# Attention and two MoE layers on one core: float32r scores for 50 of 80 items, an earlier load of block 2, logits a step later

## The chip, the cores and the metric

One core of a Trainium2 chip runs the whole program. The metric is the time of one execution in device microseconds. Before the change the median of three runs is 1098.74 us (1095.99 to 1099.82).

Engines are called by these names: TensorE (PE in the profile; PEld is its weight load, which overlaps), VectorE (DVE), ScalarE (ACT), GpSimd (POOL) and SyncE (SP), whose queue issues most of the DMA transfers. Each engine works through its own queue in order.

## What is computed

Three layers in a row, on 4 x 576 = 2304 tokens with 512 features, everything in float32:

```python
# attention, 4 batches x 8 heads x 576 tokens x 64
scores = q @ k.T / 8 + bias            # bias[h, i, j]: a small MLP of log1p|i-j| / log1p(max(i, 1))
attn = softmax(scores)                 # sums + 1e-9
x = attn @ v                           # laid out as 2304 x 512
# first MoE layer: dense, 512 -> 2048 -> 512
h = x @ w_in
y = (h * clip(h + 3, 0, 6) / 6) @ w_out
# second MoE layer: each token to the one of 8 experts with the largest logit
e = argmax(y @ w_gate)
out = gate * sigmoid(y @ w_output_gate)[e] * (relu(y @ w1[e]) @ w2[e])
```

## The kernel before, in words

**Attention.** The work is cut into 80 items. An item is a pair of heads (pr), of a unit u (a batch and four of its heads; 8 units), for a chunk c of query rows (64 rows, then four chunks of 128). Units 0 to 2 come first, interleaved over the chunks, with the computation of the bias between them (items 0 to 29). Units 3 to 7 follow, one after the other, 10 items each (items 30 to 79). A software pipeline of steps works on several items at once: `Attn.emit` writes for each step s the scores of item s (`qk`, Q0 and Q1, lines 313 to 330), the exponentials of item s-1 (`sm_exp`, line 336), its normalization (`sm_norm`, lines 342 to 345), the transposes of item s-3 (`pv_tr`, line 358, copied out of PSUM in lines 361 and 363) and the product with V of item s-4 (`pv`, lines 373 to 380, stored to `xT_d` in line 380). The order within a step is a string, `T0 S T1 X0 X1 Q0 Q1 P N T2`; at S all that was hung on this step with `side[s]` is issued: loads of q (`load_q`, line 306), K (`load_k`, line 299), V, and pieces of the MoE that start early.

The scores are fp32 matmuls, line 325: K and q of two heads lie in partitions 0 to 63 and 64 to 127, so one head uses the upper and one the lower 64 rows of the array (`tile_position=(64 * i, 0)`); each has two halves of 288 columns. Line 328 adds the bias on VectorE and takes the row's minimum of the negated scores.

**First MoE layer.** Tokens come in nine blocks of 256 (`NB`). Its matrices are held as pairs of float32r values: a high part (a copy that rounds to float32r, on ScalarE) and a low part (the subtraction, on VectorE), and each product is three float32r matmuls, high x high, high x low and low x high. The weights w_in and w_out arrive as 32 pieces of 64-bit numbers (`w_load`, line 576), each turned into such a pair by `w_steps` in four parts a to d (lines 603, 606, 609 and 610, 613 and 614). Pieces 0 to 3 are converted during attention (`w_early`, at steps 36 + 8p and the four after), the rest in `tick`, called from the loop over the matmul groups. `w_c` of piece p starts loads up to piece p+3. A block's rows are loaded by `x_load` (line 638) and split by `x_prep` (lines 656 and 657; for block 2 lines 649 and 650). `l1_` is a group of 12 matmuls of 256 columns (line 671) and its activation (lines 677 to 683), `l2_` six matmuls of 512 columns (line 701). Blocks 0 to 2 run interleaved, `seq` holding the order; groups 0 and 1 are issued already within the attention's last steps (`next(gen)`).

**Routing.** `tail` gives six parts per block: copy y out (line 714), two transposes (line 724, copied in line 725), the logits (line 730), their transposition and gate (line 738 on), the position in the expert's table (line 763 on). `tails(b, g, steps)` hangs them on matmul groups, one number of `steps` for each.

**Second MoE layer.** Slots of 128 tokens of one expert, again with float32r pairs (lines 1024 and 1052); the change doesn't touch it.

Buffers are named by tags, and a new tile under a tag waits until the tile before has been read. Tags that matter here: `K0` to `K2`, `V0` to `V2`, `xb0` to `xb3`, `cv`, `e0` to `e4` (softmax rows), `xo0` and `xo1` (attention output ahead of its store), `qh0`, `qh1`, `ql0`, `ql1`, `qraw`, `r0` and `r1`.

## Time and profile before

| | |
|---|---|
| median of three runs | 1098.74 us |
| the profiled execution | 1101.62 us |
| its span, first to last instruction | 1099.9 us |
| mean granted TensorE clock | 0.984 |
| TensorE busy | 1050.7 us (96%) |
| VectorE busy | 617.7 us (56%) |
| ScalarE busy | 539.5 us (49%) |
| GpSimd busy | 221.0 us (20%) |

The profile records one execution. "Busy" of TensorE counts from a matmul's start to its modelled end, so that matmuls which follow each other closely overlap; how fast they follow is seen from their starts in the timeline. A row of the timeline gives start, duration, engine, line and operation of one or several instructions of a kind (x8: eight of them from the first start to the last end), and in brackets the idle time of the engine before and what ended it. Attention lasts to about 386 us, the first MoE layer to about 815 us, the second to the end.

### The profile page before, as it was taken

Reading aid. Unit: us, or ns where it says so; the run is one execution under the profiler, and the core shown is the slowest. Engines: PE = TensorE matmul, PEld = TensorE weight load, DVE = VectorE, ACT = ScalarE, POOL = GpSimd, SP = SyncE. Lnnn points to the kernel's source line nnn. Section 1 sums busy time; section 2 is a strip of 40 time slices with the busy share of each in tenths; the row PEclk is TensorE's granted clock in tenths of the full one; section 3 lists DMA queues with packets and bytes.
Section 4 is the critical chain, followed back from the end, with each engine's and each line's share of the span. In section 5 each row is a group of like instructions: output and inputs, shape, how many; then the busy total and the mean of one; then the engine's idle time right before and its main releaser. Section 6 shows DMA issues by size and latency. Waiting matters only on the chain. (4 is left out here: it accounts for less than half of the span.)

```text
span 1099.9 us, 20984 instructions
## 1 busy us (share of the span) xinstructions
PE 1050.7 (96%) x7637; PEld 818.7 (74%) x7637; DVE 617.7 (56%) x1554; ACT 539.5 (49%) x1198; POOL 221.0 (20%) x273
## 2 busy tenths in 40 slices
PE   5999999999999979999999999999999989999996
PEld 2355556767777769988788888898887868777774
DVE  4887865667776757776454443436355624345320
ACT  4678777667776644554333333333343123354421
POOL 0132323434444300000010000001311243221111
PEclk9999999999999989999999999999999989999998
DMA  7555481323232143431102010110421265677841
GB/s 233 173 192 171 155 281 50 107 77 97 76 95 75 52 127 113 124 126 58 58 21 39 1 39 1 39 39 2 136 77 33 56 234 209 236 291 278 330 160 38
DMA packets 62192, 129.19 MB, mean 117 GB/s; under 512 B 13820, under 2 KB 35708, under 8 KB 59264
## 3 DMA queue, kind: packets, MB, share of 16 engines
q1 hardware_dynamic: 57424, 117.69, 32.3%
q0 software_dynamic: 4512, 9.49, 3.0%
q8 instruction: 62, 1.02, 0.4%
q10 hardware_dynamic: 144, 0.59, 0.3%
q14 instruction: 50, 0.41, 0.2%
HBM read 164.08 MB, written 14.65 MB: 163 GB/s over the span
## 5 line engine op out<-in xcount | busy, mean ns | idle before, releaser
L701 PE MATMUL acc<-wp,g 128*128 128x512 f32 x864 | 227.3, 398 | 2.1 <-issue 1.7
L671 PE MATMUL ph<-xh,wp 128*128 128x256 f32 x1024 | 207.3, 285 | 1.4 <-ACT y L714 1.2
L701 PEld LDWEIGHTS acc<-wp,g 128*128 128x128 f32 x864 | 154.4, 190 | 29.4 <-issue 2.1
L345 POOL TENSOR_SCALAR e<-e,st 128x576 f32<-128x576 f32 (+1 forms) x160 | 126.2, 801 | 246.0 <-DVE st L343 177.0
L671 PEld LDWEIGHTS ph<-xh,wp 128*128 128x128 f32 x1024 | 167.0, 189 | 11.0 <-issue 3.7
L328 DVE CUSTOM_DVE_ANT_0 e<-sc,bias 128x576 f32<-128x576 f32 (+1 forms) x160 | 116.4, 751 | 63.6 <-PE sc L325 60.9
L671 PE MATMUL ph<-xl,wp 128*128 128x256 f32 x512 | 144.6, 282 | 0.7 <-issue 0.4
L677 ACT ACTIVATE r<-ph,small 128x256 f32<-128x256 f32 x144 | 67.4, 468 | 128.8 <-PE ph L671 124.3
L336 ACT ACTIVATE e<-e,st 128x576 f32<-128x576 f32 (+1 forms) x160 | 123.0, 776 | 0.0
L678 DVE SCALAR_TENSOR_TENSOR t<-r,ph 128x256 f32<-128x256 f32 x144 | 60.3, 419 | 109.8 <-ACT r L677 109.7
L680 ACT ACTIVATE g<-t 128x256 fp32r<-128x256 f32 x144 | 60.2, 418 | 115.0 <-DVE t L678 114.0
L1024 PE MATMUL peh<-ws,xt 128*128 128x512 f32 x408 | 102.7, 405 | 5.1 <-PEq L1334 5.0
L325 PE MATMUL sc<-K,q 64*128 64x288 f32 (+1 forms) x640 | 103.0, 432 | 0.1
L358 PE MATMUL pt<-cst,e 128*128 128x128 f32 (+1 forms) x720 | 97.5, 268 | 2.9 <-ACT eT L361 1.8
L671 PEld LDWEIGHTS ph<-xl,wp 128*128 128x128 f32 x512 | 97.0, 189 | 4.1 <-DVE xl L657 0.5
L358 PEld LDWEIGHTS pt<-cst,e 128*128 128x128 f32 (+1 forms) x720 | 75.8, 141 | 31.7 <-issue 14.1
L775 POOL DMA_INDIRECT tab_d<-small x18 | 18.2, 1008 | 387.6 <-DVE small L773 353.0
L1024 PEld LDWEIGHTS peh<-ws,xt 128*128 128x128 f32 x408 | 76.9, 192 | 23.1 <-issue 5.7
L683 DVE SCALAR_TENSOR_TENSOR g<-t,g 128x256 fp32r<-128x256 f32 x144 | 61.1, 424 | 56.1 <-ACT g L680 56.1
L1052 PE MATMUL peo<-ws,ehh 128*128 128x512 f32 x272 | 86.1, 398 | 0.0
L373 PEld LDWEIGHTS po<-eT,V 128*64 128x64 f32 x1280 | 64.0, 138 | 24.8 <-issue 17.4
L373 PE MATMUL po<-eT,V 128*64 128x128 f32 (+1 forms) x1280 | 81.9, 271 | 0.0
(215 smaller groups left out, 1454.5 us busy)
## 6 DMA issues: line engine op xcount, KB each, us to landing
er<-in_we SPq DMA_DIRECT2D x46, 1024.0 KB
er<-in_we SPq DMA_DIRECT2D x86, 512.0 KB
xb<-in_xb SPq DMA_DIRECT2D x38, 512.0 KB
wraw<-in_wf SPq DMA_DIRECT2D x32, 512.0 KB
cv<-in_xb SPq DMA_DIRECT2D x11, 512.0 KB
K<-in_kT SPq DMA_DIRECT2D x8, 576.0 KB
xr<-xT_d SPq DMA_DIRECT2D x9, 512.0 KB
y_d<-y SPq DMA_DIRECT2D x18, 256.0 KB
```

The source lines that it names most:

```text
L325: nc.tensor.matmul(self.sc[i][:R, n, :288], q[d, pr, :], self.kv[u][d, pr, n * 288:(n + 1) * 288], start=True, stop=True, tile_position=(6 ...
L328: nc.vector.tensor_tensor_reduce(out=e[:R, j, :].rearrange("p (n s) -> p n s", n=2), in0=self.sc[j][:R, :, :288], in1=self.bias[c][:R, 4 * ...
L336: self.nc.scalar.activation(e[:R, j, :], e[:R, j, :], AF.Exp, scale=-1.0, bias=st[:R, j:j + 1], accum_out=st[:R, 4 + j:5 + j])
L345: nc.gpsimd.tensor_scalar(e[:R, j, :], e[:R, j, :], st[:R, 6 + j:7 + j], 1.0, op0=ALU.mult, op1=ALU.mult)
L358: nc.tensor.transpose(pt[:, i, :R], src[3 * gi + i], self.ident[:R, :R])
L373: nc.tensor.matmul(po[64 * j:64 * j + 64, :], vm[:, 2 * pr + j, kb, :], eT[:, 2 * kb + j, :], start=kb == 0, stop=False, tile_position=(0, ...
L671: nc.tensor.matmul(ph, w, x[c], start=n == 0, stop=n == 11)
L677: nc.scalar.activation(r, ph, AF.Relu, bias=self.three)
L683: nc.vector.scalar_tensor_tensor(g[:, 1], t, 1.0 / 6.0, g[:, 0].bitcast(F32), op0=ALU.mult, op1=ALU.subtract)
L701: nc.tensor.matmul(acc[t], x, w, start=f == 0 and i == 0, stop=f == 15 and i == 2)
L1024: nc.tensor.matmul(ph[:, n, :], a, w, start=c == 0 and i == 0, stop=c == 3 and i == 2)
L1052: nc.tensor.matmul(d["po"], a, w, start=f == 0 and i == 0, stop=f == 7 and i == 2)
```

## The change

The scores of units 3 to 7 (50 of the 80 items) are made of three float32r products. K and q of these units are loaded into raw buffers; `prep_k` and `prep_q` split them into high and low parts, with a copy on ScalarE and a subtraction on VectorE. K of unit 3 is loaded two steps earlier than before and split in steps 28 and 29, that of the others five and four steps ahead of their first item; q is split one step ahead of its use, from a single raw buffer, and the next load of q is issued right behind.

The rows of block 2 are loaded at step 73 together with those of blocks 0 and 1, into `cv` in place of `e4`; before, that was done in group 2 just ahead of their split. The parts of the routing of blocks 0, 1 and 2 are spaced so that the logits have a step of their own behind the second transpose. To make room, the activation's tile r takes the tags `xo0` and `xo1`, and the raw buffers of weight pieces 4 to 7 change: pieces 4 and 6 in `V1`, 5 and 7 in `V2`, and `w_c` of pieces below 6 loads one piece less ahead.

```diff
@@ class Attn
     def load_k(self, u):
         b, hf = UNITS[u]
-        self.kv[u] = self.tl(f"K{u if u < 3 else 1 - u % 2}", [2, S])
-        self.nc.sync.dma_start(self.kv[u], self.A["kT"][b, hf])
+        if u < 3:
+            self.kv[u] = self.tl(f"K{u}", [2, S])
+            self.nc.sync.dma_start(self.kv[u], self.A["kT"][b, hf])
+            return
+        if u == 3:
+            raw = [self.tl(f"xb{pr}", [S], name="kraw") for pr in range(2)]
+        else:
+            t = self.tl("K2", [2, S], name="kraw")
+            raw = [t[:, pr] for pr in range(2)]
+        for pr in range(2):
+            self.nc.sync.dma_start(raw[pr], self.A["kT"][b, hf][:, pr])
+        self.kraw[u] = raw
+
+    def prep_k(self, u, pr):
+
+        nc = self.nc
+        if pr == 0:
+            self.kv[u] = self.tl(f"K{1 - u % 2}", [2, 2, S], F32R)
+        k = self.kv[u]
+        nc.scalar.copy(k[:, 0, pr], self.kraw[u][pr])
+        nc.vector.tensor_tensor(k[:, 1, pr], self.kraw[u][pr], k[:, 0, pr].bitcast(F32), op=ALU.subtract)
 
     def load_q(self, u, c):
...
-        q = self.tl(("qh0", "qh1", "ql0", "ql1")[i % 4], [2, R], name="q")
+        q = self.tl("qraw" if u > 2 else ("qh0", "qh1", "ql0", "ql1")[i % 4], [2, R], name="q")
...
+    def prep_q(self, u, c, raw):
+        nc = self.nc
+        R = CH[c][1]
+        i = self.qj = getattr(self, "qj", -1) + 1
+        q = self.tl(("ql1", "qh0", "qh1", "ql0")[i % 4], [2, 2, R], F32R, name="q")
+        nc.scalar.copy(q[:, 0], raw)
+        nc.vector.tensor_tensor(q[:, 1], raw, q[:, 0].bitcast(F32), op=ALU.subtract)
         return q
@@ qk
-            for n in range(2):
-                for i in range(2):
-                    d = slice(64 * i, 64 * i + 64)
-                    nc.tensor.matmul(self.sc[i][:R, n, :288], q[d, pr, :], self.kv[u][d, pr, n * 288:(n + 1) * 288],
-                                     start=True, stop=True, tile_position=(64 * i, 0))
+            if u < 3:
+                parts = [(q[:, pr], self.kv[u][:, pr])]
+            else:
+
+                k = self.kv[u]
+                parts = [(q[:, a, pr], k[:, z, pr]) for a, z in ((0, 0), (0, 1), (1, 0))]
+            for m, (a, z) in enumerate(parts):
+                for n in range(2):
+                    for i in range(2):
+                        d = slice(64 * i, 64 * i + 64)
+                        nc.tensor.matmul(self.sc[i][:R, n, :288], a[d], z[d, n * 288:(n + 1) * 288],
+                                         start=m == 0, stop=m == len(parts) - 1, tile_position=(64 * i, 0))
@@ Attn.emit
+        raws = {}
+
+        def q_next(i):
+
+            if i >= n15:
+                qs[uc[i]] = self.prep_q(*uc[i], raws.pop(i))
+            if n15 - 1 <= i < len(uc) - 1:
+                raws[i + 1] = self.load_q(*uc[i + 1])
+            elif i + 2 < n15:
+                q_load(i + 2)
+
+        n15 = len(GROUPS[0]) * len(CH)
...
-            side[max(0, s0 - 1)].append(lambda i=i: q_load(i + 2))
+            side[max(0, s0 - 1)].append(lambda i=i: q_next(i))
...
-            side[first[u] - (3 if u == 3 else 9)].append(lambda u=u: self.load_k(u))
+            side[first[u] - (5 if u == 3 else 9)].append(lambda u=u: self.load_k(u))
+            for pr in range(2):
+                side[first[u] - (2 if u == 3 else 5) + pr].append(lambda u=u, pr=pr: self.prep_k(u, pr))
@@ Moe.x_load
-        raw = self.x01[:, b] if b < 2 else self.tl("e4", [4, 256], name="xr")
+        raw = self.x01[:, b] if b < 2 else self.tl("cv" if b == 2 else "e4", [4, 256], name="xr")
@@ Moe.l1_
-        r = self.tl(f"r{i % 2}", [256], name="r")
+        r = self.tl(f"xo{(i + 1) % 2}", [256], name="r")
@@ Moe.w_loads, Moe.w_c
-            self.w_load(p, f"V{(p - 3) % 3}")
+            self.w_load(p, f"V{({4: 1, 5: 2, 6: 1, 7: 2}.get(p, (p - 8) % 3))}")
...
-            self.w_loads(p + 4)
+            self.w_loads(p + (3 if p < 6 else 4))
@@ Moe.early
-        add(73, lambda: (self.x_load(0), self.x_load(1)))
+        add(73, lambda: [self.x_load(b) for b in range(3)])
@@ Moe.emit
-        tails(0, 48, (1, 2, 3, 3, 4, 5))
-        tails(1, 48, (6, 7, 8, 8, 9, 10))
-        tails(2, 48, (2, 12, 13, 13, 14, 15))
+        tails(0, 48, (1, 2, 3, 4, 5, 6))
+        tails(1, 48, (7, 8, 9, 10, 11, 12))
+        tails(2, 48, (2, 13, 14, 15, 16, 17))
...
                 if g == 2:
-                    self.x_load(2)
                     self.x_prep(2)
                     self.w_a(5)
```

## Rows read from the trace of the kernel before

**Rows 1.** By stretch: busy us (count) of PE, PEld, DVE, ACT, POOL; clock, DMA, GB/s.

```profile
300.00:371.00 71.00, 70.92 (x713) 53.44 (x710) 50.88 (x156) 50.14 (x135) 31.85 (x43) 1.00 0.29 84
385.00:420.00 35.00, 28.10 (x161) 23.80 (x160) 19.20 (x40) 14.35 (x33) 0.00 (x0) 0.85 0.41 128
```

**Rows 2.** TensorE's waits over the span: us in total, times, longest.

```profile
PE ph L671 <- ACT wp L649: 3.6, 1, 3.6
PE pl L730 <- DVE yT L725: 3.2, 4, 0.9
PE ph L671 <- DVE t L678: 2.7, 1, 2.7
```

**Rows 3.** Timeline of one item, 328 to 332 us: scores and the next ones.

```profile
328.52 1.24 PE L325 MATMUL sc<-K,q 64*128 64x288 f32 x8
...
332.11 0.79 PEld L325 LDWEIGHTS sc<-K,q 64*128 64x128 f32 x8 [0.17 <-issue]
```

**Rows 4.** The same timeline, ScalarE and VectorE.

```profile
328.67 0.48 ACT L361 COPY eT<-pt 128x384 f32<-128x384 f32 x1 [0.76 <-PE pt L358]
...
329.90 0.76 DVE L328 CUSTOM_DVE_ANT_0 e<-sc,bias 128x576 f32<-128x576 f32 x1 [0.91 <-PE sc L325]
```

**Rows 5.** Narrow timelines: the last and the first pair of a score group.

```profile
241.98 0.41 PE L325 MATMUL sc<-K,q 64*128 64x288 f32 x2
...
332.12 0.51 PE L325 MATMUL sc<-K,q 64*128 64x288 f32 x2
```

**Rows 6.** Timeline of TensorE in the first MoE layer, 420 to 424 us.

```profile
420.86 1.55 PE L701 MATMUL acc<-wp,g 128*128 128x512 f32 x6
422.25 1.58 PE L671 MATMUL ph<-wp,wp 128*128 128x256 f32 x12
423.68 0.63 PE L701 MATMUL acc<-wp,g 128*128 128x512 f32 x2
```

**Rows 7.** Page, costliest groups: busy us, mean ns, idle before.

```profile
L671 PEld LDWEIGHTS ph<-xh,wp 128*128 128x128 f32 x1024 | 167.0, 189 | 11.0 <-issue 3.7
```

**Rows 8.** ScalarE's waits over the span: us in total, times, longest.

```profile
ACT cva L603 <- DMA wraw<-in_wf: 8.8, 4, 4.4
```

**Rows 9.** Timeline, 247 to 252 us: a weight piece's load and its first use.

```profile
247.88 0.46 SPq L576 DMA_DIRECT2D wraw<-in_wf  x1
...
251.81 0.69 ACT L603 ACTIVATE cva<-wraw 128x512 f32<-128x512 f32 x1 [1.72 <-DMA wraw<-in_wf]
```

**Rows 10.** Groups by line and shape, ScalarE and VectorE: busy us, mean ns.

```profile
L680 ACT ACTIVATE g<-t 128x256 fp32r<-128x256 f32 x144 | 60.2, 418 | 115.0 <-DVE t L678 114.0 <-issue 1.0
L613 ACT CAST wp<-cvb 128x512 fp32r<-128x512 f32 x18 | 10.9, 608 | 0.0
...
L683 DVE SCALAR_TENSOR_TENSOR g<-t,g 128x256 fp32r<-128x256 f32 x144 | 61.1, 424 | 56.1 <-ACT g L680 56.1
L614 DVE TENSOR_TENSOR wp<-cvd,wp 128x512 fp32r<-128x512 f32 x14 | 9.7, 693 | 9.5 <-ACT wp L613 9.5
```

**Rows 11.** Timeline of the hand-over, 386 to 401 us: ScalarE and SP.

```profile
386.09 0.82 SPq L576 DMA_DIRECT2D wraw<-in_wf  x2
...
386.50 0.27 ACT L378 COPY xo<-po 128x128 f32<-128x128 f32 x1 [1.34 <-PE po L375]
...
387.00 0.90 SPq L380 DMA_DIRECT2D xT_d<-xo  x2
...
387.95 0.55 SPq L638 DMA_DIRECT2D xr<-xT_d  x1
...
393.61 1.14 ACT L649 CAST wp<-xr 128x512 fp32r<-128x512 f32 x2 [6.84 <-DMA xr<-xT_d]
...
398.82 0.34 SPq L576 DMA_DIRECT2D wraw<-in_wf  x1
...
400.68 0.67 ACT L603 ACTIVATE cvc<-wraw 128x512 f32<-128x512 f32 x1
```

**Rows 12.** Timeline of TensorE, 541 to 544 us: the logits of block 0.

```profile
543.01 0.64 PE L730 MATMUL pl<-yT,small 128*32 128x256 f32 x8 [0.78 <-DVE yT L725]
```

More of the change, by code (lines that the diff above doesn't have):

```diff
@@ L162, in __init__ @@
         self.ident = cst[:, 0:128]
-        self.bias, self.kv, self.v, self.lib = {}, {}, {}, {}
+        self.bias, self.kv, self.kraw, self.v, self.lib = {}, {}, {}, {}, {}
     def dram(self, name, offset, ap):
@@ L304, in load_q @@
         i = self.qi = getattr(self, "qi", -1) + 1
-        q = self.tl(("qh0", "qh1", "ql0", "ql1")[i % 4], [2, R], name="q")
+        q = self.tl("qraw" if u > 2 else ("qh0", "qh1", "ql0", "ql1")[i % 4], [2, R], name="q")
         self.nc.sync.dma_start(q, self.A["qT"][b, hf, :, :, r0:r0 + R])
+        return q
+    def prep_q(self, u, c, raw):
[5 more added lines that the diff above has]
+        nc.vector.tensor_tensor(q[:, 1], raw, q[:, 0].bitcast(F32), op=ALU.subtract)
         return q
```

## The prediction

> **What bounds the kernel now.** I read the busy time by stretch first [rows 1]. In 300 to 371 us, which is attention items like those the change touches, TensorE is busy all the time, VectorE 50.88 of 71 us and ScalarE 50.14. In 385 to 420 us, where attention hands over to the first matrix multiplication of the MoE, TensorE is busy 28.10 of 35 us and its granted clock averages 0.85. So the first stretch is bound by TensorE and the second by something that TensorE waits for. The list of TensorE's waits [rows 2] names it: 3.6 us for ScalarE's line 649 (the split of block 2's rows), 2.7 us for line 678, and 3.2 us in four waits before the logits (line 730).
>
> "Busy" alone doesn't prove that a stage is TensorE's, since matmuls overlap. The timeline of one item does [rows 3]: the score matmuls start at 328.52, the next item's weight loads at 332.11, 3.59 us later, and the idle time ahead of these is 0.17 us of "issue": they waited for no other engine. In the same item VectorE waits 0.91 us for the scores and ScalarE 0.76 us for a transpose [rows 4]. TensorE feeds them, not they TensorE. A shorter score group should therefore shorten the item.
>
> **The scores.** An item has four fp32 matmuls (two halves of 288 columns, two heads in the upper and lower 64 rows of the array). The trace shows each as two instructions, so 8. The group lasts 1.24 us [rows 3]; the last two take 0.41 us, the first two 0.51 us, their own weight load inside [rows 5]. So the last pair starts 0.83 us after the first, and the three steps between are (0.83 - 0.10) / 3 = 0.243 us each. Eight instructions one after another would need 1.94 us, so the two heads do run side by side. Four steps: 0.97 us.
>
> The change issues 3 products x 2 halves x 2 heads = 12 float32r instructions, six pairs. What a float32r instruction costs is shown in the MoE at granted clock 1.00: six of 512 columns from 420.86 to 422.25, 0.232 us each; twelve of 256 from 422.25 to 423.68, 0.119 us each [rows 6]. That is 0.46 ns a column, so 288 columns take 0.132 us, six pairs 0.79 us. Saved: 0.18 us an item, if the pairs stay side by side. If float32r ran at half the fp32 instruction's time, 0.1215 us, it would be 0.24. No row shows float32r in half the array's rows; a rival covers that.
>
> The weight loads, 12 for 8, I cost at nothing: a float32r load takes 189 ns [rows 7] while such matmuls start every 0.119 us [rows 6], so loads already run under matmuls of the same rows. The Trainium skill ("TensorE: Matmul & The Clock Gate", Part 3, The mechanism) says that a load overlaps running matmuls only where the row group differs; these rows contradict it for the full array, and by it the score group would get longer rather than shorter. That case stands among the rivals, priced from rows.
>
> Over 50 items, 9.0 us. Not all of it arrives. Four pieces of the first weights are loaded one step before ScalarE reads them, and ScalarE waits for them, 8.8 us in four waits [rows 8]; 3.93 us pass from issue to use [rows 9], so a shorter step only lengthens that wait. I take about two items off for each of the four: 42 x 0.18 = 7.6 us.
>
> **The splits this needs.** 25 chunks of q (two pieces of up to 128 columns) cost ScalarE a copy and VectorE a subtraction of 256 columns, 0.42 us each; 10 halves of K, 576 columns, about 0.61 x 576/512 = 0.68 us on ScalarE and 0.78 us on VectorE [rows 10]. Sums: ScalarE 25 x 0.42 + 10 x 0.68 = 17.3 us, VectorE 18.3 us, or 0.35 and 0.37 us an item. Both engines are busy 72% of the stretch [rows 1], 2.5 us of an item; with the addition 2.9 of the new 3.4. A q split lies ahead of the score reading, where VectorE has 0.91 us idle [rows 4]. Where a q and a K split fall in one step, VectorE's 1.2 us exceed that by some 0.3 us. That is once a unit, five units, and half as much again for subtractions queued behind a late ScalarE copy: I charge 0.6 us in place of nothing. The bounds are 0 and the whole 18.3 us. On SP, K now arrives as two transfers instead of one, and each load of q waits until the split before it has emptied the only raw buffer. Behind it stand the store of the item and, a step later, weight loads; the split is done within its step, so I cost that at nothing. If q came late, its split would hold up ScalarE and VectorE, but it is loaded two items (7 us) ahead and even the larger weight load takes 3.93 us [rows 9]. Scores net: -7.0 us, bounds -11.8 (50 x 0.24, no loss) and -3.
>
> **The hand-over.** In the kernel before, block 2's load is issued at 387.95 behind weight loads that waited for a V buffer, and ScalarE stands 6.84 us in front of line 649 until it lands [rows 11]. VectorE and ScalarE then work off a chain of weight conversions, and TensorE waits for it (2.7 us for line 678, [rows 2]). After the change the load goes out at the 74th of 80 items, over six items of 3.59 us earlier, on SP behind the loads of blocks 0 and 1 and ahead of the last stores and of all weight loads from piece 4 on; those have several items' time, so the move costs nothing there. Line 649 can start at 386.77, right after the last copy, and the chain moves up by 6.84 us. Three waits take some of this back.
> Weight piece 7 was loaded at 386.09; now its load goes out when piece 5's raw buffer is read (line 609), the place of the load at 398.82, and ScalarE wants it at the place of 400.68 [rows 11], 1.86 us later. With 3.93 us from issue to use [rows 9] ScalarE waits 2.1 us, and the activations of the MoE stand behind it on its queue.
> The activation tile r now shares the buffers xo of the attention output: the first MoE activations must wait until the last output stores have left. Those went out at 387.00 [rows 11]. How long such a store takes isn't shown; bounded by 0 and 3.93 us after issue, which leaves 0 to about 1 us for each of two waits. I take 0.35 us each, nearer to zero because the store is a quarter of the size of that load.
> Hand-over: -6.84 + 2.1 + 0.7 = -4.0 us; bounds -6.8 (no new wait) and -1 (both new waits at their worst). The half-clock matmuls after the stall I leave out: TensorE waits for the chain there either way.
>
> **The logits.** For blocks 0, 1 and 2 the logits came right behind the transposes, and TensorE waited for VectorE's copy: three of the four waits of [rows 2], 0.78 us in the one shown [rows 12]. A step between them holds about 2.9 us of matmuls [rows 6], more than the copy needs. Gain: three quarters of 3.2, rounded up for the longer ones, -2.5 us; bounds -3.0 and -1.5. The other moves (x_load's buffer, the order of V buffers after piece 8) change no step that anything waits for.
>
> **Sum.** -7.0 - 4.0 - 2.5 = -13.5 us. It is made against the profiled execution, 1101.62 us (span 1099.9 plus 1.7 around it), giving 1088.1; that execution lies 2.9 us over the median of the three runs, 1098.74. The same difference from the median gives 1085.2 us.
>
> **Rivals.**
> 1. Slower: float32r doesn't run in two halves of the array at once. For it: no row of this trace shows that. Against: the fp32 instructions do it [rows 3, 5]. Twelve steps of 0.132 are 1.58 us, 0.61 longer than now, over 50 items +30.7 us; with the rest (-6.5) 1098.7 + 24 = 1123 us. It decides at a pair step of (0.97 + 6.5/50)/6 = 0.183 us. Chance 0.11.
> 2. Slower: a weight load for the same half waits until the matmul before has left. A load inside the first matmul costs 0.10 us [rows 5], so six pairs of 0.232 are 1.39 us, +0.42 us an item, +21 - 6.5: 1113 us. This is what the page named above would make of it; rows 6 and 7 speak against. Chance 0.03.
> 3. The splits take over: VectorE and ScalarE become the bound of these items. For it, their 2.9 of 3.4 us leave little; against, the idle time ahead of the scores. Half of 18.3 us exposed cancels the scores' 7.6; left are -6.5 and +1.5: about 1094 us. Chance 0.07.
> 4. The hand-over gains nothing because the waits for piece 7 and the stores merely replace the old one: -9.5, 1089 us. This lies within my own case.
> The edit does what its words say: the units 3 to 7 are 5 x 10 = 50 items, and step 73 is the 74th.
>
> **Numbers.** My own case (0.79) spans -11.8 - 6.8 - 3.0 = -21.6 to -3 - 1 - 1.5 = -5.5 us, 1077 to 1093; the range runs to 1096 to take in rival 3. What it leaves out is 1 and 2, 0.14, and the fringe. About 0.3% (3.3 us) can be told from no change. Faster: 0.79 + 0.03 of rival 3 = 0.82; the same 0.04; slower 0.14.
>
> **What would show it.** Right: score groups with 12 instructions in about 1.0 us (last pair about 0.66 after the first, plus the first load); items near 3.4 us; no wait before line 649's successor; a new ScalarE wait of about 2 us for a raw weight tile just behind it; no TensorE wait before the logits of blocks 0 to 2. Wrong: score groups over 1.2 us, items that don't shrink while VectorE or ScalarE no longer wait for TensorE, or a TensorE wait in the hand-over as long as before.

## The result, and the profile after

| | before | after |
|---|---|---|
| median (lowest to highest), us | 1098.74 (1095.99 to 1100.15), 5 runs | 1085.26 (1083.58 to 1089.32), 5 runs |
| profiled execution, us (span) | 1101.62 (1099.9) | 1083.6 (1081.8) |
| granted clock, mean | 0.984 | 0.994 |

The ratio is 0.9882 with a 95% interval of 0.9855 to 0.991. The forecast, 1085.2 us, is met to 0.06 us. It is met because two of its terms were wrong by 3.0 us each, with opposite signs, as the stages of the two profiled executions show. A stage lasts from one start to another: of an item's score group, or of one of the groups of 12 matmuls of the first MoE layer ("group n", line 721, before 671), counted from 0; the first stage starts with the span.

| stage, us | before | after | difference | forecast |
|---|---|---|---|---|
| items 0 to 29 (not changed) | 196.34 | 194.06 | -2.28 | 0 |
| items 30 to 78 | 173.73 | 169.72 | -4.01 | -7.0 |
| item 79 to group 12 (hand-over) | 55.00 | 47.99 | -7.01 | -4.0 |
| groups 48 to 72 (logits of blocks 0 to 2) | 81.03 | 78.25 | -2.78 | -2.5 |
| groups 124 to 140 (not changed) | 51.68 | 49.40 | -2.28 | 0 |
| all the rest | 542.1 | 542.4 | +0.3 | 0 |

The two stages marked "not changed" differ by 4.56 us between the two profiled executions. All kernels below have 192.3 to 197.6 us in the first, so that difference isn't the change's. In the second they have 48.7 to 49.6 us, but all of them contain the change there; before's 51.68 us stands alone, with a granted clock of 0.97 against 1.00 in after, and whether the change has a part in it isn't shown. The 4.56 us are also how the executions stand to their medians: before's lies 2.9 us above, after's 1.7 us below. The three stages of the forecast give -13.8 us, and it said -13.5.

**The items.** The profile of after by stretch (busy us and count of PE, PEld, DVE, ACT, POOL; clock; DMA share; GB/s), for items 59 to 77 and for the hand-over, answers to [rows 1]:

```profile
296.00:361.00 65.00, 64.52 (x767) 54.27 (x763) 54.01 (x166) 51.32 (x143) 33.27 (x41) 1.00 0.36 103
379.00:412.00 33.00, 28.58 (x187) 24.97 (x183) 23.18 (x48) 17.44 (x37) 0.00 (x0) 1.00 0.39 117
```

TensorE is still busy nearly all the time in the first stretch (99%). VectorE went from 72% to 83% and ScalarE from 71% to 79%. In the hand-over the granted clock is 1.00 where it averaged 0.85. The timeline of one such item of after, which answers to [rows 3] and [rows 4], shows the new score group, the twelve weight loads under it, a q subtraction of VectorE (line 334) and the reading of the scores:

```profile
324.46 0.81 PEld L360 LDWEIGHTS sc<-K,q 64*128 64x128 f32 x12 [0.17 <-DVE st L378]
324.46 1.05 PE L360 MATMUL sc<-K,q 64*128 64x288 f32 x12
...
325.27 0.42 DVE L334 TENSOR_TENSOR q<-q,q 128x256 fp32r<-128x256 f32 x1
...
325.65 0.76 DVE L363 CUSTOM_DVE_ANT_0 e<-sc,bias 128x576 f32<-128x576 f32 x1
...
327.86 0.43 PEld L360 LDWEIGHTS sc<-K,q 64*128 64x128 f32 x6 [0.17 <-issue]
```

Twelve instructions last 1.05 us where eight lasted 1.24. The last pair starts at 325.21 (narrow timeline, the same form of row as [rows 5]):

```profile
325.21 0.30 PE L360 MATMUL sc<-K,q 64*128 64x288 f32 x2
```

That is 0.75 us behind the first pair, so a step is (0.75 - 0.10) / 5 = 0.13 us, as forecast. The next item's loads start 3.40 us after this group, behind 0.17 us of "issue". The median period of items 66 to 79 fell from 3.60 to 3.41 us.

**The waits.** TensorE's and ScalarE's waits over the span of after (total us, times, longest) answer to [rows 2] and [rows 8]:

```profile
PE sc L360 <- DVE st L363: 3.0, 8, 0.9
PE ph L721 <- DVE t L728: 2.7, 1, 2.7
PE acc L751 <- DVE t L728: 1.7, 2, 1.4
PE pl L780 <- DVE yT L775: 0.7, 1, 0.7
```

```profile
ACT cva L653 <- DMA wraw<-in_wf: 8.0, 4, 4.7
ACT r L727 <- DMA xT_d<-xo: 1.8, 2, 1.0
ACT cvc L653 <- DMA wraw<-in_wf: 1.7, 1, 1.7
```

The 3.6 us in front of the split of block 2's rows are gone, and so are three of the four waits before the logits. There is a new line on top: TensorE waits eight times, 3.0 us in all, for VectorE to read the scores (line 363). And ScalarE still waits 8.0 us in four waits for the first weight pieces.

**The hand-over.** The timeline of ScalarE in after, which answers to [rows 11], shows the waits that took the place of the 6.84 us:

```profile
376.78 0.47 ACT L727 ACTIVATE r<-ph,small 128x256 f32<-128x256 f32 x1 [0.72 <-DMA xT_d<-xo]
...
380.19 1.14 ACT L699 CAST wp<-xr 128x512 fp32r<-128x512 f32 x2
...
382.95 0.47 ACT L727 ACTIVATE r<-ph,small 128x256 f32<-128x256 f32 x1 [1.04 <-DMA xT_d<-xo]
...
390.24 0.69 ACT L653 ACTIVATE cvc<-wraw 128x512 f32<-128x512 f32 x1 [1.72 <-DMA wraw<-in_wf]
...
391.78 0.42 ACT L730 ACTIVATE g<-t 128x256 fp32r<-128x256 f32 x1 [0.48 <-DVE t L728]
```

Line 699 (before 649) waits for nothing. The two activations that write the shared buffer wait for the output stores, 0.72 and 1.04 us, and the raw weight piece is waited for 1.72 us.

### The profile page after: what moved, and what is told of

Its sections match the earlier page's. It is cut to its first block, busy times and chain, and to the rows that moved or that the text cites. A ratio compares the mean times of both kernels' runs of the same rounds, so it can differ in the third digit from the quotient of the medians.

```text
span 1081.8 us, 21444 instructions
## 1 busy us (share of the span) xinstructions
PE 1033.1 (95%) x7837; PEld 819.3 (76%) x7837; DVE 632.1 (58%) x1589; ACT 551.0 (51%) x1233; POOL 230.6 (21%) x273
## 3 DMA queue, kind: packets, MB, share of 16 engines
q8 instruction: 64, 1.05, 0.4%
## 5 line engine op out<-in xcount | busy, mean ns | idle before, releaser
L751 PE MATMUL acc<-wp,g 128*128 128x512 f32 x864 | 224.2, 395 | 1.8 <-DVE t L728 1.7
L380 POOL TENSOR_SCALAR e<-e,st 128x576 f32<-128x576 f32 (+1 forms) x160 | 135.7, 860 | 230.0 <-DVE st L378 151.6
L825 POOL DMA_INDIRECT tab_d<-small x18 | 18.3, 1017 | 378.0 <-DVE small L823 342.5
L360 PE MATMUL sc<-K,q 64*128 64x288 f32 (+1 forms) x840 | 92.8, 341 | 3.0 <-DVE st L363 3.0
L360 PEld LDWEIGHTS sc<-K,q 64*128 64x128 f32 (+1 forms) x840 | 62.8, 174 | 21.4 <-issue 9.7
```

The source lines that it names most:

```text
L360: nc.tensor.matmul(self.sc[i][:R, n, :288], a[d], z[d, n * 288:(n + 1) * 288], start=m == 0, stop=m == len(parts) - 1, tile_position=(64 * ...
L380: nc.gpsimd.tensor_scalar(e[:R, j, :], e[:R, j, :], st[:R, 6 + j:7 + j], 1.0, op0=ALU.mult, op1=ALU.mult)
L751: nc.tensor.matmul(acc[t], x, w, start=f == 0 and i == 0, stop=f == 15 and i == 2)
```

## The experiments

The question was where the scores' missing 3 us went, and where the hand-over's extra 3 came from. Where a time has no interval it is one execution, beside the kernel before on the same chip. The stages of every run, in us, by the same starts as above (a period lasts from the start of one item's score group to that of the next; "four" is the sum of the four periods that end with items 38 to 41, in which ScalarE and VectorE convert the first weight piece; "six" is that of the periods that end with items 47 to 49 and 55 to 57, with the second and the third; "period" is the median of items 66 to 79; "its clock" is the lowest granted clock in windows of 3 us behind TensorE's stalls in the hand-over, two values where it fell twice):

| run | items 30 to 78 | four | six | period | hand-over | its clock | groups 48 to 72 |
|---|---|---|---|---|---|---|---|
| before | 173.73 | 17.68 | 22.06 | 3.60 | 55.00 | 0.50, 0.56 | 81.03 |
| after | 169.72 | 17.78 | 24.66 | 3.41 | 47.99 | 1.00 | 78.25 |
| e1_k_apart | 169.37 | 17.93 | 24.04 | 3.41 | 47.60 | 1.00 | 78.26 |
| e2_w_early | 165.14 | 13.95 | 23.96 | 3.41 | 49.58 | 0.65 | 78.27 |
| e3_scores_fp32 | 172.69 | 17.09 | 21.91 | 3.60 | 50.45 | 0.55 | 78.25 |
| e4_x_load_late | 171.26 | 19.30 | 24.72 | 3.41 | 53.16 | 0.65, 0.63 | 78.25 |
| e5_w_even | 165.93 | 14.24 | 24.06 | 3.41 | 49.28 | 0.60 | 78.26 |
| e6_four_products | 181.64 | 20.22 | 24.26 | 3.68 | 48.44 | 1.00 | 78.25 |
| e7_splits_fp32 | 178.32 | 20.03 | 24.24 | 3.60 | 50.59 | 0.50 | 78.26 |
| e8_logits_close | 170.42 | 18.42 | 24.74 | 3.41 | 49.47 | 0.50 | 81.03 |
| e9_k_pool | 163.80 | 13.93 | 22.91 | 3.41 | 50.67 | 0.50 | 78.26 |
| e10_kq_pool | 164.98 | 13.83 | 23.80 | 3.41 | 49.43 | 0.50 | 78.25 |
| e11_r_apart | 164.65 | 13.94 | 23.41 | 3.41 | 48.35 | 0.65 | 78.26 |
| e12_all | 164.38 | 13.93 | 23.49 | 3.41 | 48.44 | 0.57 | 78.26 |

### The scores: what the products gain, what the splits cost

**e7_splits_fp32.** The splits stay, but the 50 items have one fp32 product of the high parts again.

```diff
-                parts = [(q[:, a, pr], k[:, z, pr]) for a, z in ((0, 0), (0, 1), (1, 0))]
+                parts = [(q[:, 0, pr].bitcast(F32), k[:, 0, pr].bitcast(F32))]
```

> All splits of q and K are kept, but the scores of units 3 to 7 are one fp32 product of the high parts; this leaves the low parts out. If the splits are hidden in ordinary items, the median period of items 66 to 79 is 3.60 us as before and the splits show only at the weight conversions: items 30 to 79 take 174 to 177 us (173.7 without splits). If they are exposed throughout, at 0.37 us of VectorE an item, the median is over 3.75 and the whole over 185.

1094.77 us against 1093.29 before. The ordinary period is 3.60 us, as before the change: there the splits cost nothing. Items 30 to 78 take 178.32 us, 4.59 more than before, and the four and the six hold all of it: 20.03 - 17.68 = 2.35 and 24.24 - 22.06 = 2.18 us. So by these two executions the splits cost 4.6 us, in the items in which a weight piece is converted and nowhere else. The part in the four is the less certain one: after, e1, e4 and e8, which are the same there, take 17.78 to 19.30 us, a spread of 1.5 us. From here to after, the same splits with the shorter products, it is 178.32 - 169.72 = 8.6 us less: that is the products' gain, 2.25 us of it in the four.

**e6_four_products.** The change with the fourth product, low by low.

```diff
-                parts = [(q[:, a, pr], k[:, z, pr]) for a, z in ((0, 0), (0, 1), (1, 0))]
+                parts = [(q[:, a, pr], k[:, z, pr]) for a, z in ((0, 0), (0, 1), (1, 0), (1, 1))]
```

> A fourth product, low x low, is added to the scores of units 3 to 7: 4 instructions, two pairs more. If these items are TensorE's and float32r pairs run side by side, the median period of items 66 to 79 grows from 3.41 by 2 x 0.13 = 0.26 to 3.67 us, and items 30 to 79 by some 11 us. If VectorE or ScalarE set the period (the splits took over), it stays under 3.5. If the two halves of a pair ran one after the other, it would grow by 0.5.

The period rose from 3.41 to 3.68 us and the stage by 11.9 us. The timeline of TensorE shows a group of 16:

```profile
335.44 1.34 PE L360 MATMUL sc<-K,q 64*128 64x288 f32 x16
```

Two more pairs make the group 0.29 us longer, 0.14 us a pair, so the two halves of the array work side by side with float32r. With 16 instructions one after another at 0.132 us the group would be over 2.1 us. And the item grows with its score group, so TensorE bounds the ordinary item.

**e3_scores_fp32.** The loads and the fp32 scores of the kernel before, with the rest of the change.

```diff
...
-            side[max(0, s0 - 1)].append(lambda i=i: q_next(i))
+            side[max(0, s0 - 1)].append(lambda i=i: q_load(i + 2))
...
-            side[first[u] - (5 if u == 3 else 9)].append(lambda u=u: self.load_k(u))
-            for pr in range(2):
-                side[first[u] - (2 if u == 3 else 5) + pr].append(lambda u=u, pr=pr: self.prep_k(u, pr))
+            side[first[u] - (3 if u == 3 else 9)].append(lambda u=u: self.load_k(u))
...
```

> The scores and loads of q and K as before, the rest of the change kept. If the parts add: items 30 to 79 take the 173.7 us of before, the hand-over gains its 6.8 us and the logits their 2.8, and the ratio to before is about 1 - 9.6/1099 = 0.991. Rival: shorter items are needed for the hand-over's gain (piece 7 and the stores come earlier relative to the rest); then under 5 us are left of it, ratio 0.994 or more.

Timed: 1086.3 us (1083.73 to 1087.17), ratio 0.9922, interval 0.9893 to 0.9952. So the change without its scores is already faster by 0.8%, clear of the noise. The times of this and of after can't be told apart (their intervals overlap); the stages can: the six take 21.91 us without splits and 24.66 with them, the period 3.60 and 3.41. The hand-over gained 4.55 us on before, not the 6.8 of the parts that add: the rival's "under 5 us" came true, while the ratio lies between the two. It took 2.5 us more than in after: 1.7 of it up to group 2, most of that a longer wait for a store (2.3 us, in after 0.72), and behind that a fall of the clock that after doesn't have (below). e7, also with fp32 scores, has the same long wait:

```profile
ACT r L677 <- DMA xT_d<-xo: 2.6, 2, 2.3
```

**e1_k_apart.** The K subtractions move to steps away from the conversions, where there are such.

```diff
-                side[first[u] - (2 if u == 3 else 5) + pr].append(lambda u=u, pr=pr: self.prep_k(u, pr))
+                side[first[u] - {3: 2, 4: 5, 5: 1, 6: 2, 7: 5}[u] + pr].append(lambda u=u, pr=pr: self.prep_k(u, pr))
```

> The splits of K for units 5 and 6 are moved from the steps in which VectorE converts weight pieces 1 and 2 to steps without. From the start of item 30's scores to that of item 79's the changed kernel takes 169.7 us (before 173.7); items 47 to 49 and 55 to 57 together take 24.7 us there (before 22.1). Theory A, the splits of K meet the weight conversions on VectorE: those six items fall to about 21.5 us, the whole to about 167. Theory B, ScalarE's wait for the landing of a weight piece sets these steps: the six stay above 24, the whole within 0.5 us of 169.7.

The stage fell by 0.35 us and the six by 0.62. But two opposite movements hide in the six. The periods that end with items 47 and 57, next to the steps that the splits left, fell from 4.44 to 3.67 us and from 4.34 to 3.41. The one that ends with item 55 grew from 3.83 to 4.80: ScalarE's wait for the third weight piece there is 2.20 us long, in after 1.19. So K's splits cost some 1.7 us where they stand beside a conversion, a part of the 4.6. What lengthened that wait isn't shown.

**e2_w_early.** The first load of each of the early weight pieces goes out a step earlier.

```diff
-                add(36 + 8 * p + k, f)
+                add(36 + 8 * p + k - (k == 0), f)
```

> The four early weight pieces are loaded a step earlier, the splits stay where they are. ScalarE's waits for them (8.0 us in four) should go. Theory A (VectorE is where the loss lies): items 47 to 49 and 55 to 57 stay above 24 us, the whole from item 30 to 79 gains at most 1.5 us, most of it at items 38 to 40. Theory B (the wait for the landing): the six fall under 22.5 us and the whole to about 166.

The stage fell by 4.6 us, most of it at the four (17.78 to 13.95). That is the place of one wait. The first row is ScalarE's timeline of after, the second that of this run:

```profile
220.96 0.66 ACT L653 ACTIVATE cva<-wraw 128x512 f32<-128x512 f32 x1 [4.75 <-DMA wraw<-in_wf]
```

```profile
217.62 0.68 ACT L653 ACTIVATE cva<-wraw 128x512 f32<-128x512 f32 x1 [0.35 <-DMA wraw<-in_wf]
```

The expectation had put part of this gain at the six; these moved by 0.7 us only. The kernel before has the same wait, 4.4 us at the longest [rows 8], and 17.68 us in the same four items: the wait is not a cost of the change, it only kept the shorter products from gaining anything there. And without the wait, the splits cost next to nothing in the four (4 x 3.41 = 13.64): the 2.35 us that e7 shows there come from splits and wait together. What is left in the six is VectorE for the most part. By stretch, this run, from the start of item 47 to that of item 50, from item 55 to item 58, and then items without a conversion:

```profile
250.60:262.10 11.50, 10.83 (x120) 9.02 (x119) 10.83 (x33) 8.09 (x22) 5.63 (x6) 1.00 0.15 37
278.90:290.70 11.80, 10.55 (x120) 8.62 (x119) 11.66 (x30) 8.65 (x23) 6.45 (x8) 1.00 0.28 74
...
322.60:336.20 13.60, 13.60 (x162) 11.48 (x160) 10.29 (x33) 10.35 (x29) 6.41 (x9) 1.00 0.13 35
```

VectorE is busy 94% and 99% of the first two and 76% of the last, and TensorE, busy all the time in the last, only 94% and 89% of the first two. (In the six's own periods, one item earlier, VectorE is busy 98% and 91%.) How this reaches TensorE, the timeline of after shows at item 48:

```profile
255.48 0.41 DVE L334 TENSOR_TENSOR q<-q,q 128x256 fp32r<-128x256 f32 x1
255.81 0.69 DVE L659 SCALAR_TENSOR_TENSOR cvb<-wraw,cvb 128x512 int32<-128x512 int32 x1
256.53 1.03 DVE L660 SCALAR_TENSOR_TENSOR cvb<-cva,cvb 128x512 int32<-128x512 int32 x1
257.49 0.75 DVE L363 CUSTOM_DVE_ANT_0 e<-sc,bias 128x576 f32<-128x576 f32 x1
258.30 0.18 PEld L360 LDWEIGHTS sc<-K,q 64*128 64x128 f32 x1 [0.64 <-DVE st L363]
```

VectorE works without a gap: the subtraction of q and two conversion steps stand ahead of the reading of the scores, and the next scores wait 0.64 us for that. The second conversion step took 1.03 us instead of its usual 0.69, beside GpSimd (last section).

One of the six periods is ScalarE's as well: the one that ends with item 55, behind the wait for the third weight piece. e2 and e11 have the same code up to there. ScalarE's waits for the early pieces, first in e2, then in e11:

```profile
ACT cva L653 <- DMA wraw<-in_wf: 1.8, 2, 1.5
```

```profile
ACT cva L653 <- DMA wraw<-in_wf: 0.9, 1, 0.9
```

With 1.5 us of wait that period is 4.06 us long, with 0.9 us 3.52. The other five of the six add up to 19.9 us in both, against 20.8 in after and 18.7 in before.

**e5_w_even.** As e2, and all steps of the early pieces one item earlier.

```diff
-                add(36 + 8 * p + k, f)
+                add(35 + 8 * p + k - (k == 0), f)
```

> The early weight pieces are converted a step earlier and loaded two steps earlier, so that the two long operations of part c (1.7 us of VectorE, lines 659 and 660) fall in even steps, away from the splits of q and the second copy of a transpose, which fall in odd ones. Items 30 to 79: 169.7 us in the changed kernel, 165.1 with the earlier load alone; at the period of undisturbed items (3.41 and so on) it would be 159.3. Theory C, VectorE is overfull in the odd steps where part c meets a q split: under 163, items 47 to 49 and 55 to 57 together (24.0 to 24.7 so far) under 22. Rival, the conversion's 2.5 us of VectorE cost the same in any step: within 0.7 of 165.1, the six above 23.5.

The six stay at 24.06 us and the stage at 165.93, though ScalarE waits for none of the early pieces any more: what e2 left isn't a wait for a load on the whole. The conversion's VectorE time costs about the same whichever of these items it stands in.

**e9_k_pool, e10_kq_pool.** If VectorE is full, its subtractions have to go to another engine. Both contain e2. e9 gives GpSimd the low part of K, e10 that of q too.

```diff
-        nc.vector.tensor_tensor(k[:, 1, pr], ...)
+        nc.gpsimd.tensor_tensor(k[:, 1, pr], ...)
... (and in e10)
-        nc.vector.tensor_tensor(q[:, 1], ...)
+        nc.gpsimd.tensor_tensor(q[:, 1], ...)
```

> On top of the earlier load of the four weight pieces, the low parts of K are computed by GpSimd instead of VectorE. Items 30 to 79 take 165.1 us with the earlier load alone, 159.3 if none is disturbed. Theory D, in the items with a weight conversion VectorE has more work than TensorE (busy 94 to 97% there): 7.8 us of VectorE go, of which the 3 us at units 5 and 6 count, so 162 to 163.5. Rival, GpSimd's operations are slow or hold up VectorE: 165 or more. The whole: about 1078 us against 1094 to 1099 of before.

> As the one before, with the low parts of q on GpSimd too. Theory D: 18.3 us of VectorE are gone, items 30 to 79 fall to about 161 us and no TensorE wait for line 363 over 1 us in all is left. Rival, GpSimd delivers q too late for the next item, behind its own normalizations (two of 0.8 us an item): the median period of items 66 to 79 rises over 3.5 us and the whole over 167.

e9: the six fell by another 1.05 us to 22.91 and the stage to 163.80, the lowest of all runs, if not to the 162 to 163.5 of theory D. e12, with the same code there, has 23.49 and 164.38. The period that ends with item 55 is what differs; the other five add up to 19.0 us in both, against 19.9 in e2 and e11, so 0.9 us of the gain is clear of that wait. Timed: 1078.5 us (1077.04 to 1083.38), ratio 0.9849, interval 0.9822 to 0.9877. e10: no further gain, 23.80 and 164.98, at an unchanged period; 1079.93 us, ratio 0.9861, interval 0.9836 to 0.9886. Neither number of its expectation came. Its trace has waits of ScalarE for the raw q tile (0.8 us) and for raw weights (up to 2.4 us) where e9 has none for q and 1.3 us at the longest for early weights; whether these alone ate the gain wasn't tried.

### The hand-over

**e4_x_load_late.** Block 2's rows are loaded where the kernel before loaded them; the rest of the change stays.

```diff
-        add(73, lambda: [self.x_load(b) for b in range(3)])
+        add(73, lambda: [self.x_load(b) for b in range(2)])
...
                 if g == 2:
+                    self.x_load(2)
                     self.x_prep(2)
```

> Block 2's rows are loaded in group 2 again, the rest of the change kept. From group 2's first matmul (line 721) to group 12's the changed kernel takes 32.0 us, before 38.9. If the early load makes the hand-over's gain, this takes 37 to 39 us with a ScalarE wait of 4 to 7 us for the rows; if the new order of the weight buffers (SP no longer stands before a V buffer) makes it, under 34 us with a wait under 2.

ScalarE's wait is back:

```profile
ACT wp L699 <- DMA xr<-xT_d: 4.8, 1, 4.8
```

The hand-over takes 53.16 us, 5.2 more than after and 1.8 less than before. The wait is 4.8 us here and was 6.84 before, 2.0 more, so these last 1.8 us go with the same wait.

How much of the 5.2 us is the wait and how much the clock, windows of 3 us tell (columns as in [rows 1]). The kernel before, at its two stalls:

```profile
390.00:393.00 3.00, 0.70 (x4) 0.22 (x2) 0.00 (x0) 0.00 (x0) 0.00 (x0) 0.96 0.99 342
393.00:396.00 3.00, 1.57 (x5) 1.28 (x6) 1.58 (x3) 2.08 (x4) 0.00 (x0) 0.50 0.02 5
396.00:399.00 3.00, 3.00 (x13) 2.71 (x12) 2.31 (x6) 1.87 (x4) 0.00 (x0) 0.50 0.00 0
...
408.00:411.00 3.00, 1.18 (x4) 0.49 (x3) 2.35 (x6) 1.86 (x4) 0.00 (x0) 1.00 0.29 115
411.00:414.00 3.00, 1.82 (x12) 1.82 (x13) 2.31 (x6) 1.52 (x3) 0.00 (x0) 0.87 0.56 157
414.00:417.00 3.00, 3.00 (x12) 2.41 (x10) 2.20 (x5) 0.89 (x2) 0.00 (x0) 0.56 0.36 82
```

After:

```profile
396.00:399.00 3.00, 1.41 (x5) 0.49 (x4) 2.35 (x6) 2.09 (x5) 0.00 (x0) 1.00 0.38 154
399.00:402.00 3.00, 1.57 (x13) 1.58 (x14) 2.31 (x6) 1.50 (x3) 0.00 (x0) 1.00 0.52 139
402.00:405.00 3.00, 3.00 (x21) 2.69 (x21) 2.44 (x6) 0.90 (x3) 0.00 (x0) 1.00 0.43 82
```

And e9_k_pool, whose hand-over is written as after's:

```profile
393.00:396.00 3.00, 1.05 (x4) 0.48 (x3) 2.31 (x6) 1.86 (x4) 0.00 (x0) 1.00 0.27 109
396.00:399.00 3.00, 1.93 (x9) 1.93 (x10) 2.35 (x6) 1.51 (x3) 0.00 (x0) 0.56 0.57 173
399.00:402.00 3.00, 3.00 (x11) 2.52 (x11) 2.18 (x5) 0.89 (x2) 0.00 (x0) 0.50 0.36 105
```

The first stall of before, and the fall of the clock to 0.50 (the level of 1.2 GHz) behind it, are gone in all runs with the early load. The second stall is still there in all. Behind it the clock falls in some executions and not in others: a busy window then holds 11 or 12 matmuls instead of 21. With after's buffers and loads the hand-over took 47.99, 47.60 and 48.44 us where it didn't fall (after, e1, e6; mean 48.0), and 49.58, 49.28, 49.47, 50.67 and 49.43 where it did (e2, e5, e8, e9, e10; mean 49.7). (e7's 50.59 us are left aside for its fp32 scores and its longer store wait.) So after's profiled execution is one of the luckier, by 1.7 us between the means, though the five spread over 1.4 us among themselves. Like with like, both with the fall behind the second stall (before is one execution), the change takes the hand-over from 55.0 to 49.7 us, -5.3, and the late load alone brings it back to 53.2. What decides whether the clock falls no run tells.

**e11_r_apart.** As e2, and two of the first activations write a buffer that no store reads.

```diff
-        r = self.tl(f"xo{(i + 1) % 2}", [256], name="r")
+        r = self.tl("r0" if i in (1, 2) else f"xo{(i + 1) % 2}", [256], name="r")
```

> On top of the earlier load of the weight pieces, the activation tile r of matmul groups 1 and 2 gets a buffer of its own instead of the attention output's. ScalarE's two waits for the stores at the hand-over (1.8 us) go. If they lie on the chain that sets the hand-over, item 79 to matmul group 12 (49.6 us with the earlier load alone, 48.0 in the changed kernel) falls by 1.5 us or more; if the wait for piece 7 swallows them, by under 0.7.

The waits for the stores are gone. The hand-over is 48.35 us, and 48.44 in e12 with the same buffer, both with the fall of the clock; the five runs with it and with the store waits have 49.28 to 50.67. In e8 and e9 the view puts these idle times of ScalarE (0.97 and 0.91 us for the longer one) down to TensorE, whose matmuls had ended 1.4 us or more before the activation started. So the stores cost some 1.3 us (49.7 - 48.4), by the nearest pair 0.8, between the two numbers of the expectation. Timed: 1079.84 us, ratio 0.9859, interval 0.9835 to 0.9883.

### The logits, and all together

**e8_logits_close.** The steps of the tails as before.

```diff
-        tails(0, 48, (1, 2, 3, 4, 5, 6))
-        tails(1, 48, (7, 8, 9, 10, 11, 12))
-        tails(2, 48, (2, 13, 14, 15, 16, 17))
+        tails(0, 48, (1, 2, 3, 3, 4, 5))
+        tails(1, 48, (6, 7, 8, 8, 9, 10))
+        tails(2, 48, (2, 12, 13, 13, 14, 15))
```

> The logits of blocks 0 to 2 right behind the transposes again, the rest of the change kept. From matmul group 48 to group 72: 78.25 us in the changed kernel, 81.03 before. If the spacing alone made that gain, 81.0 within 0.2 and TensorE waits of 2.5 us in three before the logits; if it came from elsewhere, 78.3.

The stage goes back to 81.03 us, the value before, and TensorE's waits return:

```profile
PE pl L780 <- DVE yT L775: 3.2, 4, 0.9
```

**e12_all.** e9 and e11 together.

> The earlier load of the four weight pieces, K's low parts on GpSimd and r's own buffer for groups 1 and 2 together. If they add: items 30 to 79 in 163.8 us and from item 79 to matmul group 12 48.4 us or less (50.7 with K on GpSimd alone, 48.0 in the changed kernel); ratio to before 0.983 to 0.985 (the changed kernel: 0.988). If the hand-over takes back what attention gains, 0.987 or more.

Timed: 1076.92 us (1075.59 to 1083.67) against 1093.82 before on the same chip, ratio 0.985, interval 0.9827 to 0.9874. The two add up nearly as expected: 164.38 us in items 30 to 78, 48.44 in the hand-over. It has the lowest median of all, but in ratio e9, e11 and e12 can't be told from each other; they lie at 0.985 to 0.986, after at 0.988 with an overlapping interval. By the stages the gain over after is 5 to 6 us in items 30 to 78, 3.8 of it the wait taken away by e2.

## Why the prediction was right, and where it was wrong

**The float32r pair: right.** Forecast 0.132 us a pair; the narrow timeline gives 0.13 and e6 0.14. Rivals 1 and 2 (1123 and 1113 us) fall with this. The Trainium skill ("TensorE: Matmul & The Clock Gate", Part 3, The mechanism) says in one line that a load overlaps running matmuls only where the row group differs; another line of that section allows it for the background weight buffer too. Here twelve loads and six pairs, each half loaded again for every pair, fit into 1.05 us, and the weight loads left no stall between the pairs: in half the array, too, the trace does not agree with the first of these lines.

**The scores' gain: right, as far as it can be told.** The forecast took 0.18 us off 42 items, 7.6 us. Between e7 and after it was 8.6 us, but 2.25 of these lie in the four, where runs of the same code spread over 1.5 us; the missing 1 us isn't clear of that. (Its bound of -11.8 us is a slip: 50 x 0.24 is 12.0.)

**The splits: the step that failed.** "I charge 0.6 us in place of nothing" was worked out from the steps where a q and a K split meet, and it doesn't follow from its own terms: 0.3 us in five units, and half as much again, is 2.25 us, which would have made the scores' net -5.4. But those steps were the wrong ones, too. The companion that mattered was a third one, the weight conversion. In an ordinary item the cover named, VectorE's 0.91 us before the scores, was there: the period of e7 didn't move. In the ten items of the four and the six it was not, and 4.6 us were exposed (e7): 2.2 in the six, where VectorE is full (94% and 99% of two stretches in e2; moving the subtractions or the splits of K away gains time, e9 and e1) and where in one period the wait for the third weight piece has a part; and 2.4 in the four, where runs of the same code spread over 1.5 us, ScalarE stands before the first weight piece, and where e2, without that wait, shows almost nothing exposed. The average of 72% busy of [rows 1] hid this: it covers items 59 to 78 of before, in which VectorE is busy 80% around the conversion of the last early piece (items 60 to 64) and 69% behind it. So the scores net -4.0 us instead of -7.0. Rival 3 was right in its mechanism, in a fifth of the items: 4.6 of the 18.3 us it feared, not half. The "two items off for each of four waits" were also only partly so: it was mainly one wait, the first, that took away the gain of its items.

**The hand-over: the second step that failed.** The old wait went as forecast, 6.84 us to nothing, and e4 brings 4.8 us of it back. The new wait for piece 7 came near its forecast size, 1.72 us (2.1); the stores' two were longer than theirs, 0.72 and 1.04 (0.35 each, bounds 0 to about 1). But they don't add up to time as "-6.84 + 2.1 + 0.7" has it. Like with like the stage fell by 5.3 us; with 6.84 gained and 1.3 lost to the stores (e11), only 6.84 - 5.3 - 1.3 = 0.2 us are left for the wait for piece 7, and more only if the vanished first fall of the clock gave time as well. Against that speaks e4, which has the fall behind both stalls: it takes 3.5 us more than the mean of 49.7 for a wait of 4.8 us. The 1.3 us between are what the stores cost, whose longer wait is gone there, and nothing is left for the fall. Means of one and of five executions that spread over 1.4 us carry no finer account than this. Where the wait for piece 7 went is not shown: VectorE went on with its chain meanwhile, and ScalarE's next wait for VectorE was 0.48 us long, against up to 1.8 in that stretch; but waits of 0.48 us also stand where ScalarE had waited for nothing before. No run loads piece 7 earlier, which needs another buffer. The other 1.7 us of the 7.0 are the second fall of the clock, which was absent in this execution. "The half-clock matmuls after the stall I leave out: TensorE waits for the chain there either way" held for the fall behind the first stall at most, and not for that behind the second, where the comparison of the runs with it and without it gives some 1.7 us.

**The logits: right.** -2.5 forecast, -2.78 found, three of four waits, and e8 gives them back exactly.

**The sum.** Errors of +3.0 and -3.0 us cancelled in the profiled executions. The range, 1077 to 1096 us, held the time, but the agreement to 0.06 us is luck. The two stages are those of single executions, too: runs with after's code in them have 169.7 to 171.3 us in items 30 to 78 and 47.6 to 50.7 in the hand-over. Part of it is luck of the execution, too: the second of the two errors would have been -1.3 us with the fall of the clock that most other runs have.

## What to carry to other kernels

Before costing added work at nothing, look for the stretch in which the engine that takes it is fullest, not at its average over the stage: here work that was free in 40 items cost some 4.6 us (e7) in ten that also had conversions. Waits on one engine need not add up to time: of three new ones, 3.5 us in all, some 1.5 us are found in the stage by the means above. Ask for each new wait which old one it may replace. And a wait for a load that was issued one step too late hides the gain of everything around it, so it is worth moving first (e2: 3.8 us by one step).

## What the runs showed of the hardware

- Float32r matmuls of 64 rows run two at a time, in the upper and lower half of the array, at 0.13 to 0.14 us a pair of 288 columns, loads included (after and e6).
- GpSimd takes 1.41 us for the subtraction of 576 columns that takes VectorE 0.75. The operation rows of e9 and of after (shortest, median, longest ns):

```profile
L318 POOL TENSOR_TENSOR K<-kraw,K x10: 1407/1410/1838, 191.3 to 319.5; 128x576 fp32r<-128x576 f32 x10
```

```profile
L318 DVE TENSOR_TENSOR K<-kraw,K x10: 744/751/1178, 189.1 to 322.0; 128x576 fp32r<-128x576 f32 x10
```

  The Trainium skill ("GPSIMD Engine Reference", 4.1 Engine selection) puts GpSimd at about twice VectorE's time for operations with two inputs; these rows give 1.9.
- The two engines slow each other down in some of their operations. In after, the same conversion step takes 0.69 us where GpSimd is idle, and up to 1.12 where it works:

```profile
L660 DVE SCALAR_TENSOR_TENSOR cvb<-cva,cvb x18: 691/692/1118, 228.5 to 494.9; 128x512 int32<-128x512 int32 x18
L660 DVE SCALAR_TENSOR_TENSOR cvd<-cvc,cvd x14: 691/692/695, 386.5 to 498.6; 128x512 int32<-128x512 int32 x14
```

  The one of 1.03 us at 256.53 ran while the second of two operations of GpSimd's line 380 did, and these two took 2.19 us where a single one takes 0.75:

```profile
254.84 2.19 POOL L380 TENSOR_SCALAR e<-e,st 128x576 f32<-128x576 f32 x2 [1.04 <-DVE st L378]
...
259.39 0.75 POOL L380 TENSOR_SCALAR e<-e,st 128x576 f32<-128x576 f32 x1 [2.37 <-DVE st L378]
```

  Not every operation is slowed: line 659 at 255.81, also beside GpSimd, took its usual 0.69 us. The page of the Trainium skill named above (8. Key points) names such contention for VectorE instructions with two inputs from SBUF, which these are.
- The same stall of TensorE, in kernels that differ only elsewhere, is followed by a fall of the granted clock to 0.50 (1.2 GHz) in some executions and by none in others, and this is worth some 1.7 us here. A single profile of each kernel would have put it down to the change.
